# LSH attention and two feed-forwards: the feed-forwards in passes of 512 tokens instead of 768, with the gemms two steps apart

## The chip, the cores and the metric

One core of a Trainium2 chip. The metric is the device time of one execution in microseconds, the median of three runs.

## What is computed

Attention over 2 batches, 8 heads, 768 tokens and a head size of 64, in which a query sees the keys that hash to its own bucket; then two feed-forwards over all 1536 tokens, 512 to 2048 to 512 features, the first with a sigmoid-approximated gelu, the second with mish. All in fp32.

```python
mask = q_bucket[:, :, :, None] == k_bucket[:, :, None, :]
scores = np.where(mask, scale * np.matmul(q, k.transpose(0, 1, 3, 2)), -1e9)
attn = np.exp(scores - np.max(scores, axis=-1, keepdims=True))
x = np.matmul(attn / attn.sum(-1, keepdims=True), v)      # heads side by side: 1536 x 512
h = x @ w_in;  x = (h * (1 / (1 + np.exp(-1.702 * h)))) @ w_out
h = x @ w2_in; x = (h * np.tanh(log1p(exp(h)))) @ w2_out
```

## The kernel before

The order of every engine's instructions is written out by hand; no scheduler moves anything. Each value that a gemm of the feed-forward takes is split in two parts, hi (rounded to the type fp32r, in which TensorE multiplies) and lo (the rest, rounded too), and a product is three matmuls: hi by hi, hi by lo, lo by hi.

**Attention** runs in 96 steps (`NSTEP`), 16 heads of 6 blocks of 128 queries. A step does the scores of one block (`qk`, L355, PE), a clamp with its row minimum (`clamp`, L368, DVE), the exponential (`expo`, L379, ACT), and for an earlier step six transposes (`trp`, L414, PE), their hi and lo parts (L421 on ACT, L426 on DVE) and the product with v (`pv`, L438 and L439, PE). POOL prepares the operands of heads to come, and for each pair of heads sums and scales the output (`x_out`, L462 and L463) and splits it (`x_split`, x_hi and L469 for x_lo) into the x tiles of the feed-forward. `at(step, f)` hangs such extra work on a step.

**Weights** come as 64 tiles of 128 x 512, 32 for each feed-forward: for each f of 16 (blocks of 128 of the 2048 hidden features) one tile for each gemm. They are loaded as 64-bit numbers (`wload`, L101, issued by SP, three raw buffers) and made into hi and lo by `wsplit`: a scaled copy on ACT (L110), three integer instructions on DVE (L112, L114, L116), a rounding on ACT (L125) and a subtraction on DVE (L127; on POOL for tiles made under attention). `wgo(k, n)` issues the next n of these six for tile k. The first `NPRE` = 3 tiles are made under attention, one per 12 steps, the others by the steps of the feed-forward, as `conv` says: two per step in the first pass over the tokens and again in the second pass, where the tiles of the second feed-forward take the place of the first one's.

**A feed-forward** (m = 0, 1) makes two passes (b), one per batch of 768 tokens, of 16 steps (f). A step computes `gemm_in` (L159): h, 128 hidden features by 768 tokens, in two banks of 384 columns (`ps_h`, two buffers); then `act`: the activation twice on ACT (L590 rounded to gh, L591 in place) and gl on DVE (L592), which is what frees the bank; then `gemm_out` of the step before, which adds to six y banks. In the first feed-forward w is the stationary operand and the tokens move, 512 (L619) and 256 (L622) columns at a time, 24 matmuls; in the second gh and gl are stationary and w moves (L608), 18 matmuls of 512 columns. After the last f, y is copied out: into x_hi and x_lo of the next feed-forward (`x_next`), or stored (`y_store`). The two halves of h of step 0 are computed between the last steps of attention, in eight parts.

The last pair of heads of attention has its `x_out` and `x_split` in the first steps of the feed-forward; its tokens are needed in the second pass.

Of the kernel before, what the change touches and what calls it, by code (L numbers as in the profile page):

```python
# [36 lines left out]
def lsh_attention_moe_kernel(  # L37
# [18 lines left out]
    HS = S // 2  # L56
    NW0 = 1
    XO = 11
    NPRE = 3
# [20 lines left out]
    xpool = ctx.enter_context(tc.tile_pool(name="xpool", bufs=2 * B))  # L80
# [3 lines left out]
    for b in range(B):  # L84
        x_hi.append(xpool.tile([P, KD, S], F32R, tag="x", name="x_hi"))
        x_lo.append(xpool.tile([P, KD, S], F32R, tag="x", name="x_lo"))
# [17 lines left out]
    def wsplit(k, sub):  # L104
# [13 lines left out]
        pi = 0 if f < NW0 + (j == 0) else 1 if f < NW1 else 2  # L118
        nb = (NW0, NW1 - NW0, KF - NW1)[pi]
        if j == 0 and pi < 2:  # L120
            nb += 1 - 2 * pi
# [22 lines left out]
    steps = [(m, b, f) for m in range(2) for b in range(B) for f in range(KF)]  # L144
# [3 lines left out]
    def gemm_in(i, t, k0=0, k1=KD):  # L148
        m, b, f = steps[i]
        if k0 == 0:  # L150
            h_t[i, t] = mps["h"].tile([P, HS], F32, tag="h", name="h")
        h = h_t[i, t]
        wh, wl = w_t[m, f, 0]
        ct = slice(t * HS, (t + 1) * HS)
        n = 3 * k0
        for kk in range(k0, k1):
            wk = slice(kk * P, (kk + 1) * P)
            for a, x in ((wh, x_hi[b]), (wh, x_lo[b]), (wl, x_hi[b])):
                nc.tensor.matmul(  # L159
                    h, a[:, wk], x[:, kk, ct], start=(n == 0), stop=(n == 3 * KD - 1)  # L160
                )
                n += 1

    def attention():
        with ExitStack() as es:
# [359 lines left out]
            for i in range(NSTEP + PVLAG):  # L525
                if i == NSTEP:
                    es_s.close()
                    mps["h"] = ctx.enter_context(
                        tc.tile_pool(name="ps_h", bufs=2, space=PSUM, side="right")
# [32 lines left out]
                for part in range(max(0, 2 * (i - NSTEP)), min(2 * (i - NSTEP) + 2, 2 * KD)):  # L562
                    gemm_in(0, part // KD, part % KD, part % KD + 1)
# [6 lines left out]
    def moe():  # L570
        with ExitStack() as es:
            gp = es.enter_context(tc.tile_pool(name="gp", bufs=2))
            wpools[1] = es.enter_context(tc.tile_pool(name="w1", bufs=NW1 - NW0))
            ps_y = es.enter_context(tc.tile_pool(name="ps_y", bufs=1, space=PSUM))
            NH = KF * B
            N = len(steps)
            A0, A1 = 512, S - 512
# [3 lines left out]
            def act(i, t):  # L581
                if t == 0:
                    gh = gp.tile([P, S], F32R, tag="gh", name="gh")
# [76 lines left out]
            for i in range(N + 1):  # L660
                if i == NH:
                    load_table(SET_MISH)
# [93 lines left out]
```

## Time and profile before

| | us |
|---|---|
| median of 3 runs | 794.1 (793.56 to 794.52) |
| the profiled execution, its time | 795.07 |
| the profiled execution, its span | 793.3 |
| PE busy in it | 767.4 |
| DVE, ACT, POOL busy in it | 443.2, 400.3, 175.4 |

Attention takes the first 250 us, the two feed-forwards the rest. The busy time of PE contains overlap: a matmul is shown from its start to its modelled end, and the next one starts before that. What a matmul costs is read from the distance of two starts. The granted clock is the share of 2.4 GHz at which TensorE ran in a stretch; it is 1.00 nearly everywhere.

### The profile page before, as it was taken

Reading aid. Unit: us, or ns where it says so; the run is one execution under the profiler, and the core shown is the slowest. Engines: PE = TensorE matmul, PEld = TensorE weight load, DVE = VectorE, ACT = ScalarE, POOL = GpSimd, SP = SyncE. Lnnn points to the kernel's source line nnn. Section 1 sums busy time; section 2 is a strip of 40 time slices with the busy share of each in tenths; the row PEclk is TensorE's granted clock in tenths of the full one; section 3 lists DMA queues with packets and bytes.
Section 4 is the critical chain, followed back from the end, with each engine's and each line's share of the span. In section 5 each row is a group of like instructions: output and inputs, shape, how many; then the busy total and the mean of one; then the engine's idle time right before and its main releaser. Section 6 shows DMA issues by size and latency. Waiting matters only on the chain.

```text
span 793.3 us, 11713 instructions
## 1 busy us (share of the span) xinstructions
PE 767.4 (97%) x4336; PEld 705.2 (89%) x4336; DVE 443.2 (56%) x861; ACT 400.3 (50%) x864; POOL 175.4 (22%) x155
## 2 busy tenths in 40 slices
PE   5999999999997999999999999999999999999998
PEld 4999999887786999999999999999999899899996
DVE  6888888889986966765277677671111112111111
ACT  5889888887887545444344454461212213122122
POOL 7867867765821200000000000000000000000000
PEclk9999999999999899999999999999999999999999
DMA  6464464654220433333034333300000002000002
GB/s 164 133 159 109 133 153 123 160 157 128 62 67 21 159 132 114 128 133 107 1 107 133 133 119 122 131 28 1 1 0 1 1 1 80 0 1 1 1 1 79
DMA packets 23977, 65.13 MB, mean 82 GB/s; under 512 B 4048, under 2 KB 6192, under 8 KB 23920
## 3 DMA queue, kind: packets, MB, share of 16 engines
q1 hardware_dynamic: 23920, 64.39, 27.4%
q8 instruction: 34, 0.56, 0.3%
q14 instruction: 23, 0.19, 0.1%
HBM read 49.38 MB, written 3.19 MB: 66 GB/s over the span
## 4 chain that ended last, share of the span: by engine, by line
PE 85%; ACT 7%; DVE 3%; issue 2%; DMA 2%; POOL 1%; SPq 0%; DVEq 0%; ACTq 0%; POOLq 0%
PE h L159 34%; PE y L608 17%; PE y L619 11%; PE y L622 6%; PE pt L414 5%; PE s L355 5%; ACT p L379 3%; ACT pth L421 3%; PE u L438 2%; PE u L439 2%; PE prep L266 2%; DVE ptl L426 1%; POOL qx L254 1%; DVE p L368 1%; DMA kn<-in_kt_dram 1%
## 5 line engine op out<-in xcount | busy, mean ns | idle before, releaser
L592 DVE TENSOR_TENSOR gl<-h,gh 128x384 fp32r<-128x384 f32 x128 | 71.3, 557 | 290.2 <-ACT h L591 290.0
L590 ACT ACTIVATE gh<-h 128x384 fp32r<-128x384 f32 x128 | 63.0, 492 | 325.0 <-PE h L159 325.0
L159 PE MATMUL h<-x_hi,wh 128*128 128x384 f32 x512 | 172.7, 337 | 5.3 <-DVE gl L592 5.3
L159 PE MATMUL h<-x_hi,wl 128*128 128x384 f32 x512 | 172.5, 337 | 0.0
L159 PE MATMUL h<-x_lo,wh 128*128 128x384 f32 x512 | 172.4, 337 | 0.0
L426 DVE TENSOR_TENSOR ptl<-pt,pth 128x384 fp32r<-128x384 f32 x192 | 97.8, 550 | 31.5 <-ACT pth L421 31.1
L159 PEld LDWEIGHTS h<-x_hi,wh 128*128 128x128 f32 x512 | 97.0, 189 | 8.1 <-DVE gl L592 5.6
L159 PEld LDWEIGHTS h<-x_lo,wh 128*128 128x128 f32 x512 | 97.0, 190 | 1.2
L159 PEld LDWEIGHTS h<-x_hi,wl 128*128 128x128 f32 x512 | 97.0, 189 | 0.0
L379 ACT ACTIVATE p<-p,mn 128x768 f32<-128x768 f32 x96 | 90.5, 943 | 12.1 <-DVE p L368 11.9
L421 ACT CAST pth<-pt 128x384 fp32r<-128x384 f32 x192 | 82.6, 483 | 23.6 <-PE pt L414 22.8
L414 PE MATMUL pt<-ident,p 128*128 128x128 f32 x576 | 84.8, 276 | 7.7 <-DVE ptl L426 4.0
L368 DVE TENSOR_SCALAR_CACHE_REDUCE p<-s 128x768 f32<-128x768 f32 x96 | 90.1, 940 | 0.4 <-PE s L355 0.3
L414 PEld LDWEIGHTS pt<-ident,p 128*128 128x128 f32 x576 | 67.0, 140 | 20.4 <-ACT p L379 8.3
L608 PE MATMUL y<-wh,gl 128*128 128x512 f32 x192 | 75.3, 392 | 0.0
L608 PE MATMUL y<-wl,gh 128*128 128x512 f32 x192 | 75.2, 392 | 0.0
L608 PE MATMUL y<-wh,gh 128*128 128x512 f32 x192 | 74.7, 389 | 0.0
L438 PE MATMUL u<-pth,vv 128*128 128x384 f32 x192 | 65.6, 341 | 0.9 <-ACT ul L456 0.9
L439 PE MATMUL u<-ptl,vv 128*128 128x384 f32 x192 | 64.6, 337 | 0.0
L591 ACT ACTIVATE h<-h 128x384 f32<-128x384 f32 x128 | 62.4, 488 | 0.0
L355 PE MATMUL s<-kh,qx 128*128 128x384 f32 x192 | 56.0, 372 | 0.0
L355 PE MATMUL s<-kb,qb 128*128 128x384 f32 x192 | 50.2, 341 | 0.2 <-ACT kb L320 0.2
(91 smaller groups left out, 1247.7 us busy)
## 6 DMA issues: line engine op xcount, KB each, us to landing
raw<-in_wt_dram SPq DMA_DIRECT2D x64, 512.0 KB, 3.2
kn<-in_kt_dram SPq DMA_DIRECT2D x16, 384.0 KB, 6.1
qn<-in_qt_dram SPq DMA_DIRECT2D x16, 192.0 KB, 4.5
vn<-in_vt_dram SPq DMA_DIRECT2D x8, 384.0 KB, 5.2
rb<-scr SPq DMA_DIRECT2D x16, 192.0 KB, 3.4
out_dram<-ob SPq DMA_DIRECT2D x12, 256.0 KB, 2.1
qx<-qk_m SPq DMA_DIRECT2D x15, 192.0 KB, 3.3
qb<-qk_m SPq DMA_DIRECT2D x15, 192.0 KB, 2.7
```

Of the source, the lines that this page charges most:

```text
L159: nc.tensor.matmul(h, a[:, wk], x[:, kk, ct], start=(n == 0), stop=(n == 3 * KD - 1))
L355: nc.tensor.matmul(s[:, f, :HS], a[:, c], bb[:, f * HS : (f + 1) * HS], start=st, stop=not st,)
L368: nc.vector.tensor_scalar(sb, s[:, :, :HS], NEG, None, ALU.min, ALU.min, accum_out=mn)
L379: nc.scalar.activation(p, p, AF.Exp, bias=mn, scale=-1.0, accum_out=z_t[n][:, t : t + 1],)
L414: nc.tensor.transpose(ptile[:, j * P : (j + 1) * P], p_t[3 * g + j][:, t * P : (t + 1) * P], ident,)
L421: nc.scalar.copy(hi, ptile[:, :HS])
L426: nc.vector.tensor_sub(lo, ptile[:, :HS], rnd(hi))
L438: nc.tensor.matmul(ut[:, :HS], vv[:, t, :], hi, start=(t == 0), stop=False)
L439: nc.tensor.matmul(ut[:, :HS], vv[:, t, :], lo, start=False, stop=(t == NT - 1))
L592: nc.vector.tensor_sub(gl[:, ct], h, rnd(gh[:, ct]))
L608: nc.tensor.matmul(y[j], x[:, tj], w, start=(first and n == 0), stop=(last and n == 2))
L619: nc.tensor.matmul(y0, w[:, wj], x[:, :A0], start=(first and n == 0), stop=(last and n == 2))
```

## The change

The feed-forwards take the 1536 tokens in three passes of 512 (`CH`, `NCH`). A step's h is one bank of 512 columns, and there are four such banks; y is four banks of 512. Every matmul of the feed-forward has 512 columns: 12 for the first gemm and 12 for the second, in 96 steps. The second gemm runs two steps behind the first (`OLAG`), and the first gemms of steps 0 and 1 are computed between the last steps of attention. Five weight tiles are made under attention, from steps 32, 44, 56, 68 and 80 (before: three, from 56, 68 and 80). In the feed-forward the first pass makes two tiles per step in a new interleaving, the third pass three per two steps. `x_split` cuts a batch where a pass begins or ends, at 512 tokens of the first batch and 256 of the second, so that it issues four POOL instructions instead of two.

```diff
+    CH = 512
+    NCH = NTOK // CH
...
-    NPRE = 3
+    NPRE = 5
...
-        wlist += [(m, 0, 0), (m, 1, 0)]
+        wlist += [(m, 0, 0), (m, 1, 0), (m, 2, 0)]
         for f in range(KF):
-            wlist += [(m, f, 1)] + [(m, f + 2, 0)] * (f + 2 < KF)
+            wlist += [(m, f, 1)] + [(m, f + 3, 0)] * (f + 3 < KF)
...
-    steps = [(m, b, f) for m in range(2) for b in range(B) for f in range(KF)]
+    steps = [(m, c, f) for m in range(2) for c in range(NCH) for f in range(KF)]
...
-            h_t[i, t] = mps["h"].tile([P, HS], F32, tag="h", name="h")
+            h_t[i] = mps["h"].tile([P, CH], F32, tag="h", name="h")
...
-            for a, x in ((wh, x_hi[b]), (wh, x_lo[b]), (wl, x_hi[b])):
+            for a, x in ((wh, x_hi[c]), (wh, x_lo[c]), (wl, x_hi[c])):
                 nc.tensor.matmul(
-                    h, a[:, wk], x[:, kk, ct], start=(n == 0), stop=(n == 3 * KD - 1)
+                    h, a[:, wk], x[:, kk], start=(n == 0), stop=(n == 3 * KD - 1)
                 )
...
-                pcopy(x_hi[b][:, hp], ul)
-                nc.gpsimd.tensor_sub(x_lo[b][:, hp], ul, rnd(x_hi[b][:, hp]))
+                t0, t1 = b * S, (b + 1) * S
+                while t0 < t1:
+                    c, o = divmod(t0, CH)
+                    n = min(CH - o, t1 - t0)
+                    xh = x_hi[c][:, hp, o : o + n]
+                    src = ul[:, t0 - b * S : t0 - b * S + n]
+                    pcopy(xh, src)
+                    nc.gpsimd.tensor_sub(x_lo[c][:, hp, o : o + n], src, rnd(xh))
+                    t0 += n
...
-                        tc.tile_pool(name="ps_h", bufs=2, space=PSUM, side="right")
+                        tc.tile_pool(name="ps_h", bufs=4, space=PSUM, side="right")
...
-                    gemm_in(0, part // KD, part % KD, part % KD + 1)
+                    gemm_in(part // KD, part % KD, part % KD + 1)
...
-            gp = es.enter_context(tc.tile_pool(name="gp", bufs=2))
+            gp = es.enter_context(tc.tile_pool(name="gp", bufs=3))
...
+            OLAG = 2
...
+            act(0)
+            wgo(conv(2)[0], 1)
+            for i in range(2, N + OLAG):
...
+                if i < N:
+                    gemm_in(i)
+                k1, k2 = (conv(i) + [None, None])[:2]
+                if k1 is not None:
+                    wgo(k1, 2)
+                    for k in conv(i - 1)[1:]:
+                        wgo(k, 1)
+                    wgo(k1, 1)
+                    wfetch(k1 + 4)
...
+                if i - 1 < N:
+                    act(i - 1)
+                if k2 is not None:
+                    wgo(k2, 1)
+                if k1 is not None:
+                    wgo(k1, 1)
+                if k2 is not None:
+                    wgo(k2, 2)
+                if k1 is not None:
+                    wgo(k1, 1)
+                if k2 is not None:
+                    wgo(k2, 1)
+                    wfetch(k2 + 4)
+                for k in conv(i + 1)[:1]:
+                    wgo(k, 1)
+                if k2 is not None:
+                    wgo(k2, 1)
+                gemm_out(i - OLAG)
```

`gemm_out` of the change has one loop for both feed-forwards: for j of 4, three matmuls of 512 columns into y[j], w stationary in the first, gh and gl in the second; `act` works on 512 columns at once.

How the order moves is seen best behind attention. DVE before, from the last copy of attention's row sums on (raw, wb, wl: a weight tile on its way; gl: the activation's low part):

```order
L402 COPY zt<-prep 6x128
L112 TENSOR_SCALAR raw<-raw 128x512
L114 SCALAR_TENSOR_TENSOR raw<-wb,raw 128x512
L116 SCALAR_TENSOR_TENSOR wb<-wb,raw 128x512
L112 TENSOR_SCALAR raw<-raw 128x512
L114 SCALAR_TENSOR_TENSOR raw<-wb,raw 128x512
L592 TENSOR_TENSOR gl<-h,gh 128x384
L116 SCALAR_TENSOR_TENSOR wb<-wb,raw 128x512
L127 TENSOR_TENSOR wl<-wb,wh 128x512
L592 TENSOR_TENSOR gl<-h,gh 128x384
L127 TENSOR_TENSOR wl<-wb,wh 128x512
```

The same place of DVE in the change, where the five instructions have become L114, L116, L118, L128 and L596:

```order
L402 COPY zt<-prep 6x128
L596 TENSOR_TENSOR gl<-h,gh 128x512
L114 TENSOR_SCALAR raw<-raw 128x512
L116 SCALAR_TENSOR_TENSOR raw<-wb,raw 128x512
L118 SCALAR_TENSOR_TENSOR wb<-wb,raw 128x512
L596 TENSOR_TENSOR gl<-h,gh 128x512
L114 TENSOR_SCALAR raw<-raw 128x512
L116 SCALAR_TENSOR_TENSOR raw<-wb,raw 128x512
L128 TENSOR_TENSOR wl<-wb,wh 128x512
L118 SCALAR_TENSOR_TENSOR wb<-wb,raw 128x512
```

The gl of step 0 has moved ahead of all conversion work, and from the second tile on the wl of one tile stands between two instructions of the next.

POOL in the middle of attention, in the change, from a head's operands to the next v operand (before, x_hi and x_lo were one row of 768 columns each, and the first wl stood 24 steps later):

```order
L258 TENSOR_TENSOR qk_m<-kn,kh 64x768
L77 TENSOR_SCALAR x_hi<-ul 128x512
L475 TENSOR_TENSOR x_lo<-ul,x_hi 128x512
L77 TENSOR_SCALAR x_hi<-ul 128x256
L475 TENSOR_TENSOR x_lo<-ul,x_hi 128x256
L128 TENSOR_TENSOR wl<-wb,wh 128x512
L77 TENSOR_SCALAR vv<-vn 128x6x64
```

Two rows have become four, and the wl of the first weight tile stands behind them.

## Rows read from the trace of the kernel before

**Rows 1.** The page, part 1: busy us (share) xinstructions of each engine.

```profile
PE 767.4 (97%) x4336; PEld 705.2 (89%) x4336; DVE 443.2 (56%) x861; ACT 400.3 (50%) x864; POOL 175.4 (22%) x155
```

**Rows 2.** Waits of PE, whole span: us in total, times, longest us.

```profile
PE h L159 <- DVE gl L592: 5.3, 1, 5.3
```

**Rows 3.** Timeline of PE, both feed-forwards: start us, us, engine, line, operation, x.

```profile
286.57 0.34 PE L159 MATMUL h<-x_hi,wh 128*128 128x384 f32 x1
...
294.89 0.34 PE L159 MATMUL h<-x_hi,wh 128*128 128x384 f32 x1
...
706.45 0.39 PE L608 MATMUL y<-wh,gh 128*128 128x512 f32 x1
...
710.58 0.33 PE L159 MATMUL h<-x_hi,wh 128*128 128x384 f32 x1
```

**Rows 4.** Timeline of PE, between attention and feed-forward: start us, us.

```profile
253.34 0.27 PE L396 MATMUL prep<-ident,z 128*6 128x128 f32 x1
258.87 0.69 PE L159 MATMUL h<-x_hi,wh 128*128 128x384 f32 x1 [5.26 <-DVE gl L592]
...
264.48 0.39 PE L159 MATMUL h<-x_hi,wl 128*128 128x384 f32 x1
264.71 0.33 PE L159 MATMUL h<-x_hi,wh 128*128 128x384 f32 x1
```

**Rows 5.** Timelines of POOL, DVE and ACT over the same wait.

```profile
253.53 1.81 POOL L462 TENSOR_TENSOR ul<-ul,uh 128x768 f32<-128x768 f32 x1 [13.77 <-ACT ul L456]
...
253.86 1.76 DVE L112 TENSOR_SCALAR raw<-raw 128x512 uint32<-128x512 uint32 x1
...
254.60 0.47 ACT L590 ACTIVATE gh<-h 128x384 fp32r<-128x384 f32 x1
...
258.27 0.55 DVE L592 TENSOR_TENSOR gl<-h,gh 128x384 fp32r<-128x384 f32 x1
```

**Rows 6.** Timeline of DVE: the clamps of attention steps 43, 55, 67, 79, 91.

```profile
109.44 0.94 DVE L368 TENSOR_SCALAR_CACHE_REDUCE p<-s 128x768 f32<-128x768 f32 x1
...
137.76 0.95 DVE L368 TENSOR_SCALAR_CACHE_REDUCE p<-s 128x768 f32<-128x768 f32 x1
...
168.61 0.95 DVE L368 TENSOR_SCALAR_CACHE_REDUCE p<-s 128x768 f32<-128x768 f32 x1
...
201.03 0.95 DVE L368 TENSOR_SCALAR_CACHE_REDUCE p<-s 128x768 f32<-128x768 f32 x1
...
232.08 0.94 DVE L368 TENSOR_SCALAR_CACHE_REDUCE p<-s 128x768 f32<-128x768 f32 x1
```

**Rows 7.** Timelines of POOL and DVE, step 73 of attention.

```profile
187.47 1.84 POOL L469 TENSOR_TENSOR x_lo<-ul,x_hi 128x768 fp32r<-128x768 f32 x1
...
187.75 2.12 DVE L116 SCALAR_TENSOR_TENSOR wb<-wb,raw 128x512 uint32<-128x512 uint32 x1
```

**Rows 8.** Timeline of DVE, one weight tile in the first feed-forward.

```profile
309.01 0.69 DVE L127 TENSOR_TENSOR wl<-wb,wh 128x512 fp32r<-128x512 f32 x1
309.62 0.42 DVE L112 TENSOR_SCALAR raw<-raw 128x512 uint32<-128x512 uint32 x1
310.14 0.70 DVE L114 SCALAR_TENSOR_TENSOR raw<-wb,raw 128x512 uint32<-128x512 uint32 x1
310.87 0.69 DVE L116 SCALAR_TENSOR_TENSOR wb<-wb,raw 128x512 uint32<-128x512 uint32 x1
311.48 0.42 DVE L112 TENSOR_SCALAR raw<-raw 128x512 uint32<-128x512 uint32 x1
```

**Rows 9.** Waits of SP's DMA queue from 257 to 345 us: total, times, longest.

```profile
SPq L101 <- DVE wb L116: 80.6, 23, 5.0
```

**Rows 10.** The page, part 6: the weight loads, KB each, median us to landing.

```profile
raw<-in_wt_dram SPq DMA_DIRECT2D x64, 512.0 KB, 3.2
```

**Rows 11.** Stretches: us, busy us (x) of PE, PEld, DVE, ACT, POOL; PEclk, DMA share, GB/s.

```profile
257.00:260.00 3.00, 1.13 (x4) 1.13 (x4) 2.90 (x5) 1.39 (x3) 1.66 (x1) 0.63 0.51 191
440.00:460.00 20.00, 20.00 (x117) 18.69 (x116) 14.40 (x27) 10.47 (x22) 0.00 (x0) 1.00 0.38 131
```

More of the change, by code (lines that the diff above doesn't have):

```diff
@@ L78, in rnd @@
         return ap.bitcast(F32)
-    xpool = ctx.enter_context(tc.tile_pool(name="xpool", bufs=2 * B))
+    xpool = ctx.enter_context(tc.tile_pool(name="xpool", bufs=2 * NCH))
     wr = ctx.enter_context(tc.tile_pool(name="wr", bufs=3))
     x_hi, x_lo = [], []
-    for b in range(B):
-        x_hi.append(xpool.tile([P, KD, S], F32R, tag="x", name="x_hi"))
-        x_lo.append(xpool.tile([P, KD, S], F32R, tag="x", name="x_lo"))
+    for c in range(NCH):
+        x_hi.append(xpool.tile([P, KD, CH], F32R, tag="x", name="x_hi"))
+        x_lo.append(xpool.tile([P, KD, CH], F32R, tag="x", name="x_lo"))
     wpools = {0: ctx.enter_context(tc.tile_pool(name="w0", bufs=NW0))}
@@ L117, in wsplit @@
         yield
[L118 to L121, printed above, removed]
+        n0 = NW0 + 3 * (j == 0)
+        pi = 0 if f < n0 else 1 if f < NW1 else 2
+        nb = (n0, NW1 - n0, KF - NW1)[pi]
         hi = wpools[pi].tile([P, DM], F32R, tag=f"wh{j}", name="wh", bufs=nb)
@@ L599, in gemm_out @@
                 if first:
-                    y_t[m, b] = [
-                        ps_y.tile([P, 512], F32, tag=f"y{j}", name=f"y{j}") for j in range(6)
-                    ]
-                y = y_t[m, b]
-                if m == 1:
-                    for j in range(NT):
-                        tj = slice(j * P, (j + 1) * P)
-                        for n, (x, w) in enumerate(((gh, wh), (gh, wl), (gl, wh))):
-                            nc.tensor.matmul(
-                                y[j], x[:, tj], w, start=(first and n == 0), stop=(last and n == 2)
-                            )
-                        if last:
-                            y_store(b, j)
-                    return
+                    y_t[m, c] = [
+                        ps_y.tile([P, CH], F32, tag=f"y{j}", name=f"y{j}") for j in range(KD)
+                    ]
@@ L614, in gemm_out @@
+                y = y_t[m, c]
                 for j in range(KD):
[L615 to L618 removed]
+                    js = slice(j * P, (j + 1) * P)
+                    for n, (x, w) in enumerate(((gh, wh), (gh, wl), (gl, wh))):
                         nc.tensor.matmul(
[L620 to L628 removed]
@@ L629, in gemm_out @@
-                    if last:
-                        x_next(b, j, slice(0, A0), y0)
-                        if j % 2:
-                            for jj in (j - 1, j):
-                                o = (jj % 2) * A1
-                                x_next(b, jj, slice(A0, S), y[KD + j // 2][:, o : o + A1])
-            def x_next(b, j, c, y):
-                nc.scalar.copy(x_hi[b][:, j, c], y)
-                nc.vector.tensor_sub(x_lo[b][:, j, c], y, rnd(x_hi[b][:, j, c]))
+                            y[j],
@@ new lines, in gemm_out @@
+                            w[:, js] if m == 0 else x[:, js],
+                            x if m == 0 else w,
+                            start=(first and n == 0),
+                            stop=(last and n == 2),
+                        )
+                    if last and m == 0:
+                        nc.scalar.copy(x_hi[c][:, j], y[j])
+                        nc.vector.tensor_sub(x_lo[c][:, j], y[j], rnd(x_hi[c][:, j]))
+                    elif last:
+                        y_store(c, j)
```

108 lines of the change are left out of this document (34 added, 74 removed).

## The prediction

> **What bounds the kernel now.** I read the page's busy times first, then PE's waits, then timelines where a wait ends or a step repeats. PE is busy 97% of the span [rows 1], so a change gains only by giving PE less work, by closing a wait of PE's, or it loses by making PE wait. Behind attention PE has one wait of size: 5.3 us, ended by DVE's gl of line 592 [rows 2]. From there to the end it runs without a gap, so the feed-forward costs what its matmuls cost. In attention PE isn't alone: a step is as long as the loop PE, ACT, DVE and back, and DVE's clamp of line 368, one per step, is the clock of that loop [rows 6].
>
> **Fewer, wider matmuls.** In the first feed-forward one step lasts from 286.57 to 294.89, 8.32 us [rows 3]: 24 matmuls of 384 columns, 12 of 512 and 12 of 256, together 18,432 columns. At 2.4 GHz these stream for 7.68 us, so 0.64 us over 48 matmuls is left, 13.3 ns each. In the second feed-forward 18 matmuls of 512 columns take from 706.45 to 710.58, 4.13 us against 3.84 of streaming: 16 ns each. The columns stay what they are. The matmuls go from 32 x 48 + 32 x 42 = 2880 to 96 x 24 = 2304. 576 fewer at 13.3 ns is **-7.7 us**, all of it on PE's path, and I take the 13.3 since most of the removed ones are of 384 and 256 columns.
>
> The Trainium skill (TensorE: Matmul & The Clock Gate, section "Wait — 56ns, not 53.3ns?") gives a warm back-to-back matmul a fixed cost of only 2.5 ns beside its columns. By that the term would be 576 x 2.5 ns = 1.4 us; the rows here show five times as much, in two kinds of step, and they decide.
>
> **The wait behind attention.** PE ends its last attention work, the small transpose of 253.34, and next starts at 258.87, after 5.26 us of idling [rows 4]. It wants an h bank; there are two, and the first is held until gl of step 0 has read it. That gl starts at 258.27, since DVE has five conversion instructions ahead of it, the first stretched to 1.76 us by a POOL instruction that began at 253.53 [rows 5] (0.42 where nothing is in the way [rows 8]). After the idling the clock is at the lower level: the 18 matmuls that start from 258.87 to 264.48 stand 5.61 us apart in all, where 17 intervals of a 384-column matmul (160 ns of streaming and 13.3) are 2.95. So the wait costs 5.26 + 2.66 = 7.9 us.
>
> After the change PE has work there: steps 0 and 1 are computed inside attention's last steps, there are four h banks, and gemm_in of step 2 (12 x 0.227 = 2.72 us) needs only a third bank and a weight tile made under attention. PE's tail of attention has 24 matmuls of 512 instead of 384 columns, 1.3 us more, so that it ends at about 254.6 on the old time scale, and gemm_in of step 2 ends at 257.3. ACT's gelu of step 0 stands directly behind the last u copies, without the two REBIAS instructions of before; they took it to 254.60 [rows 5], so even 1 us later it ends by 256, and gl(0), first in DVE's queue now, by 256.3. That is 1 us ahead of gemm_out(0). The next weight needed, second-gemm tile of step 1, is the first tile that the feed-forward makes itself; PE wants it at 262.7, two PE blocks later, and the seven DVE instructions up to its wl take 4.3 us by rows 8, out of 6. The wait goes: **-7.9 us**.
>
> **Two more weight tiles under attention.** The clamps of steps 43, 55, 67, 79 and 91 give four stretches of 12 steps [rows 6]: 28.32 us without a conversion, then 30.85, 32.42 and 31.05 with one each. So the first costs 2.53 us, the second 4.10, the third 2.73. The new ones begin 24 and 12 steps earlier, at the same place in the pattern of 12 steps (32 and 44 instead of 56). With five in a row I take the old first price for the first, the old last for the last, and the middle one three times: 2.53 + 3 x 4.10 + 2.73 = 17.56 against 9.36, +8.2 us.
>
> From this a part goes back. In step 73 L116 takes 2.12 us instead of 0.69 [rows 7, 8]: it starts 0.28 behind POOL's x_lo of line 469 and ends 0.56 behind that one's end, as if it had begun only then. The change cuts x_hi and x_lo into pieces of 512 and 256 columns. The first x_lo piece is two thirds of 1.84 us and starts some 0.25 earlier, because x_hi's piece before it is shorter: it ends about 0.8 us earlier, and L116 could run between the two pieces. I give 0.75 for each of the four conversions that meet an x_split (in the last of the old ones there was no such meeting): -3.0. Together **+5.2 us**. Ends: +8.2 if the cut helps nothing; +2.1 if the two new tiles cost the lowest seen price less the help (2 x 1.8) and the old ones get theirs (2 x 0.75).
>
> **The first pass of the feed-forward.** A step of PE shrinks from 8.32 us to 24 x 0.227 = 5.44, while two tiles per step still have to be made in it. By the starts in rows 8, DVE's instructions follow each other in 0.61 (wl), 0.52 (L112), 0.73 (L114, whose consumer is next) and 0.61 (L116). In the new order a wl stands between L114 and L116, so that I count 0.61 there: 2.35 per tile, and with 0.61 for a gl of 512 columns 5.31 us per step. DVE is then 98% full but not the bound, and the five tiles made beforehand and the two steps between the gemms absorb a late instruction. POOL's last x_out and x_split fall into the first steps and can hold DVE up. For this and for the four y banks that the next pass takes over at once from copies (a gemm_in of 2.72 us lies between) I allow **+1.5 us**. In the last pass of the first feed-forward three tiles are made per two steps, 3.5 us of DVE per 5.44; the second feed-forward makes none. The end (last copy and store) is unchanged.
>
> **Sum.** -7.7 - 7.9 + 5.2 + 1.5 = -8.9 us. The profiled execution (795.07 us, 1.8 of it outside its span of 793.3) would become 786.2. It lies 1.0 above the median of the runs, 794.1, on which the forecast is made: **785.2 us**. What a measurement can tell from no change is about 0.2%, 1.6 us.
>
> **Rivals.**
>
> *DVE becomes the bound of the first pass.* At whole durations instead of start distances a tile is 0.42 + 0.70 + 0.69 + 0.69 = 2.50 us [rows 8], a step 2 x 2.50 + 0.69 = 5.69: 0.25 over PE's 5.44, 3.3 us in 13 steps. If three of POOL's last instructions also stretch one of DVE's as in rows 5 (1.76 instead of 0.42), that is 4.0 more. Less the 1.5 allowed: 785.2 + 5.8 = 791.0. For it: DVE has only 2% left. Against: rows 8 show the overlap of neighbours. Chance 0.16.
>
> *The change doesn't close the wait.* PE stops at gemm_out(0) or (1) instead, for gl(0) or the first weight tile made late, long enough for the clock to fall as in rows 4: +7.9, 793.1 us. Against: gl(0) stands first now. Chance 0.07.
>
> *A matmul's fixed cost is no cost of the matmul.* If the 13.3 ns belonged to the columns (a weight load or an operand read that goes on beside them and grows with them), wider matmuls would keep all of it: +7.7, 792.9 us. Rows 3 speak against it, three widths with about the same rest per matmul. Chance 0.03. (The 2.5 ns of the Trainium skill, same page and section, would end near it, at 791.5 us.)
>
> *Slower: the weight loads.* The first pass needs 24 more loads of 512 KB in some 13 x 5.44 = 71 us, 177 GB/s; in steady state they ran at 131 [rows 11]. At that rate they take 24 x 0.524 MB / 131 = 96 us, PE waits 25 us in pieces, 810 us. It turns the sign where less than about 155 GB/s comes. Against: SP's loads waited 80.6 us in 23 waits for DVE to free a buffer [rows 9], so 131 is what was asked, one lands in 3.2 us [rows 10] with three buffers to turn in 8.2 us, and 191 GB/s stands in one stretch [rows 11]. Chance 0.06.
>
> **How the numbers follow.** The forecast has 0.68; its own range, from the attention ends (-3.1, +3.0) and from no stall at all (-1.5), is 781 to 788.5. With the DVE case, 0.16, it holds 0.84: 781 to 791. Faster by over 0.2% (below 792.5) are the forecast and the DVE case: 0.84. Within 0.2% are the wait that stays and the fixed-cost case: 0.10. Slower is the load case: 0.06.
>
> **What would show it.** Right, step by step: 2304 feed-forward matmuls with starts 227 ns apart and steps of 5.44 us; no PE wait over 1 us between attention and feed-forward and a granted clock of 1.00 there; stretches of 12 attention steps of 30 to 32 us from step 31 on, and a last clamp about 5 us later; L116's counterpart at 1.3 to 1.5 us instead of 2.1. Wrong: PE waits for wl or gl that repeat every step of the first pass, raw loads landing in 5 us or more, or an attention that ends over 8 us later.

## The result, and the profile after

| | before | after |
|---|---|---|
| median of 4 runs | 794.25 us (793.56 to 794.52) | 784.40 us (782.43 to 787.02) |
| ratio, 95% interval | | 0.9879 [0.9858, 0.9901] |
| the profiled execution: time, span | 795.07, 793.3 | 783.52, 781.5 |

The changed kernel is 1.2% faster, 9.9 us by the medians; 785.2 was forecast. A second set of four runs of the same kernel gave 784.04. In the profiled executions it is 11.5 us (795.07 to 783.52), since the one of the kernel before lies above its four runs and that of the changed kernel below its median. In the changed kernel the load of a raw tile stands in line 103, the three integer instructions in L114, L116 and L118, the rounding in L126, wl in L128, x_lo in L475, gl in L596, and the second gemm in L612.

The page after, part 1, against [rows 1]:

```profile
PE 758.0 (97%) x3760; PEld 642.4 (82%) x3760; DVE 434.6 (56%) x823; ACT 397.6 (51%) x796; POOL 184.4 (24%) x173
```

The 576 matmuls are gone (4336 to 3760). PE is as full as before, so the span followed PE's work and PE's waits. The waits of PE after, whole span, against [rows 2] (us in total, times, longest):

```profile
PE s L355 <- DMA kb<-mk: 1.3, 2, 1.1
PE h L159 <- DVE wl L128: 0.9, 1, 0.9
```

The wait of 5.3 us for gl has gone, and in the feed-forward one of 0.9 us for a wl has come. New, too, are the 1.3 us in attention for small transfers (kb <- mk, a mask). The clamps of steps 31, 43, 55, 67, 79, 91 and 95 (the last) in DVE's timeline after, against [rows 6]:

```profile
81.17 0.95 DVE L368 TENSOR_SCALAR_CACHE_REDUCE p<-s 128x768 f32<-128x768 f32 x1
...
111.26 0.95 DVE L368 TENSOR_SCALAR_CACHE_REDUCE p<-s 128x768 f32<-128x768 f32 x1
...
142.92 0.95 DVE L368 TENSOR_SCALAR_CACHE_REDUCE p<-s 128x768 f32<-128x768 f32 x1
...
174.56 0.94 DVE L368 TENSOR_SCALAR_CACHE_REDUCE p<-s 128x768 f32<-128x768 f32 x1
...
206.38 0.94 DVE L368 TENSOR_SCALAR_CACHE_REDUCE p<-s 128x768 f32<-128x768 f32 x1
...
236.55 0.95 DVE L368 TENSOR_SCALAR_CACHE_REDUCE p<-s 128x768 f32<-128x768 f32 x1
...
246.42 0.95 DVE L368 TENSOR_SCALAR_CACHE_REDUCE p<-s 128x768 f32<-128x768 f32 x1
```

The last clamp of before stood at 241.71. So attention ends **4.7 us later**, and what follows it takes 781.5 - 246.42 = 535.1 us instead of 793.3 - 241.71 = 551.6: **16.5 us less**. Together -11.8, the difference of the two spans.

A step of PE in each feed-forward, from one step's first matmul of the second gemm to the next one's (timeline of PE after):

```profile
301.63 0.39 PE L612 MATMUL y<-gh,wh 128*128 128x512 f32 x1
...
307.07 0.39 PE L612 MATMUL y<-gh,wh 128*128 128x512 f32 x1
...
704.19 0.39 PE L612 MATMUL y<-wh,gh 128*128 128x512 f32 x1
...
709.63 0.39 PE L612 MATMUL y<-wh,gh 128*128 128x512 f32 x1
```

Both are 5.44 us for 512 tokens, 8.16 for 768. In the first feed-forward a step of 768 tokens took 8.32 [rows 3]. In the second it took 8.31, from this row of the kernel before to the 710.58 of [rows 3]:

```profile
702.27 0.33 PE L159 MATMUL h<-x_hi,wh 128*128 128x384 f32 x1
```

Over 32 steps each that is 5.1 + 4.8 = 9.9 us of the 16.5. The other 6.6 us lie between attention and the feed-forward, where PE's timeline after answers to [rows 4]:

```profile
258.84 0.40 PE L159 MATMUL h<-x_hi,wl 128*128 128x512 f32 x1
259.07 0.27 PE L396 MATMUL prep<-ident,z 128*6 128x128 f32 x1
259.10 0.48 PE L159 MATMUL h<-x_hi,wh 128*128 128x512 f32 x1
...
261.94 0.39 PE L612 MATMUL y<-gh,wh 128*128 128x512 f32 x1
...
270.10 0.39 PE L159 MATMUL h<-x_hi,wh 128*128 128x512 f32 x1
...
271.57 0.50 PE L159 MATMUL h<-x_hi,wl 128*128 128x512 f32 x1 [0.86 <-DVE wl L128]
...
277.15 0.39 PE L159 MATMUL h<-x_hi,wh 128*128 128x512 f32 x1
```

Behind the small transpose the first gemm of step 2 goes on at once, and at 261.94 the second gemm of step 0 follows. The next rows are those of DVE and POOL over the stretch, against [rows 5]:

```profile
260.50 0.69 DVE L596 TENSOR_TENSOR gl<-h,gh 128x512 fp32r<-128x512 f32 x1 [0.84 <-ACT h L595]
...
264.77 2.33 DVE L128 TENSOR_TENSOR wl<-wb,wh 128x512 fp32r<-128x512 f32 x1
...
269.74 1.78 DVE L128 TENSOR_TENSOR wl<-wb,wh 128x512 fp32r<-128x512 f32 x1
```

```profile
264.43 2.13 POOL L463 TENSOR_TENSOR ul<-ul,rb 128x768 f32<-128x768 f32 x1 [3.67 <-DMA rb<-scr]
...
269.36 1.61 POOL L475 TENSOR_TENSOR x_lo<-ul,x_hi 128x512 fp32r<-128x512 f32 x1
```

gl of step 0 ends 0.75 us before PE wants it. Then two of DVE's wl meet POOL's instructions and last 2.33 and 1.78 us instead of 0.69: the second one is the wait of 0.86. That step takes 7.05 us (270.10 to 277.15) instead of 5.44, and the two ahead of it 0.1 us too much: the first pass loses 1.7 us, and every later step takes 5.44. In the kernel before, the wait took 5.3 us and the step behind it 11.06 (258.87 to 269.93) instead of 8.32, 8.0 us lost in all, so 6.3 of the 6.6 us are accounted for. The stretches of the first pass (as in [rows 11]) show how full DVE is:

```profile
260.00:280.00 20.00, 19.04 (x83) 15.06 (x82) 18.77 (x27) 10.70 (x19) 7.04 (x6) 1.00 0.40 140
280.00:300.00 20.00, 20.00 (x90) 16.57 (x89) 19.17 (x35) 13.71 (x24) 0.00 (x0) 1.00 0.60 189
300.00:320.00 20.00, 20.00 (x90) 16.54 (x90) 19.27 (x35) 13.30 (x24) 0.00 (x0) 1.00 0.60 207
```

DVE is busy 96% and PE 100%, and the loads run at up to 207 GB/s: neither the DVE rival nor the load rival came about.

### The profile page after: what moved, and what is told of

Read it like the earlier page. It is cut to its first block, busy times and chain, and to the rows that moved or that the text cites. A ratio compares the mean times of both kernels' runs of the same rounds, so it can differ in the third digit from the quotient of the medians.

```text
span 781.5 us, 10532 instructions
## 1 busy us (share of the span) xinstructions
PE 758.0 (97%) x3760; PEld 642.4 (82%) x3760; DVE 434.6 (56%) x823; ACT 397.6 (51%) x796; POOL 184.4 (24%) x173
## 4 chain that ended last, share of the span: by engine, by line
PE 79%; DVE 6%; ACT 5%; DMA 3%; POOL 3%; issue 3%; SPq 1%; DVEq 0%; POOLq 0%; ACTq 0%
PE y L612 33%; PE h L159 32%; PE s L355 4%; PE pt L414 4%; ACT p L379 2%; PE u L438 2%; PE u L439 2%; ACT pth L421 2%; PE prep L266 2%; POOL qx L254 1%; DMA vn<-in_vt_dram 1%; DMA kb<-mk 1%; DVE ptl L426 1%; DVE p L368 1%; DVE z L391 1%
## 5 line engine op out<-in xcount | busy, mean ns | idle before, releaser
L596 DVE TENSOR_TENSOR gl<-h,gh 128x512 fp32r<-128x512 f32 x96 | 66.2, 690 | 267.2 <-ACT h L595 266.8
L594 ACT ACTIVATE gh<-h 128x512 fp32r<-128x512 f32 x96 | 57.3, 597 | 256.1 <-PE h L159 255.5
L159 PE MATMUL h<-x_hi,wl 128*128 128x512 f32 x384 | 149.6, 389 | 0.9 <-DVE wl L128 0.9
L159 PE MATMUL h<-x_hi,wh 128*128 128x512 f32 x384 | 149.5, 389 | 0.0
L159 PE MATMUL h<-x_lo,wh 128*128 128x512 f32 x384 | 149.4, 389 | 0.0
L426 DVE TENSOR_TENSOR ptl<-pt,pth 128x384 fp32r<-128x384 f32 x192 | 97.8, 550 | 30.7 <-ACT pth L421 30.2
L159 PEld LDWEIGHTS h<-x_hi,wl 128*128 128x128 f32 x384 | 72.1, 188 | 16.3 <-DVE wl L128 1.3
L159 PEld LDWEIGHTS h<-x_lo,wh 128*128 128x128 f32 x384 | 72.0, 188 | 14.7
L612 PE MATMUL y<-gh,wl 128*128 128x512 f32 x192 | 74.8, 390 | 0.1
L612 PE MATMUL y<-gh,wh 128*128 128x512 f32 x192 | 74.7, 389 | 0.0
L612 PE MATMUL y<-wh,gh 128*128 128x512 f32 x192 | 74.7, 389 | 0.0
L612 PE MATMUL y<-wl,gh 128*128 128x512 f32 x192 | 74.7, 389 | 0.0
L612 PE MATMUL y<-gl,wh 128*128 128x512 f32 x192 | 74.7, 389 | 0.0
L612 PE MATMUL y<-wh,gl 128*128 128x512 f32 x192 | 74.7, 389 | 0.0
## 6 DMA issues: line engine op xcount, KB each, us to landing
out_dram<-ob SPq DMA_DIRECT2D x12, 256.0 KB, 2.0
```

What stands on the lines that cost most here:

```text
L159: nc.tensor.matmul(h, a[:, wk], x[:, kk], start=(n == 0), stop=(n == 3 * KD - 1))
L426: nc.vector.tensor_sub(lo, ptile[:, :HS], rnd(hi))
L594: nc.scalar.activation(gh, h, fn)
L596: nc.vector.tensor_sub(gl, h, rnd(gh))
L612: nc.tensor.matmul(y[j], w[:, js] if m == 0 else x[:, js], x if m == 0 else w, start=(first and n == 0), stop=(last and n == 2),)
```

## The experiments

Eleven further kernels were run, and the changed kernel once more. Each ratio is against the kernel before, run beside it. The ranges behind the medians are the lowest and highest run.

### Does the cost belong to the matmul or to its columns?

`e2_halves_second_ff`: the changed kernel, with the first gemm of the second feed-forward in halves, the same columns in 576 more matmuls.

```diff
-                nc.tensor.matmul(h, a[:, wk], x[:, kk], start=..., stop=...)
+                for o in (0, 256) if m else ():
+                    nc.tensor.matmul(h[:, o : o + 256], a[:, wk], x[:, kk, o : o + 256], start=..., stop=...)
+                if m == 0:
+                    nc.tensor.matmul(h, a[:, wk], x[:, kk], start=..., stop=...)
```

> The changed kernel, with each matmul of the first gemm of the second feed-forward (576 of 512 columns, a part in which no weight tile is made) cut into two of 256: 576 matmuls more, the same columns. Theory (13.3 ns for each matmul whatever its width): a step of the second feed-forward goes from 5.44 to 5.60 us, the run is 7.7 us longer than the changed kernel, about 792. Rival (2.5 ns for each matmul, the rest belongs to the columns): 1.4 us longer. Second rival (at 256 columns the load of the stationary operand, 188 ns long, no longer hides beside the stream): more than 15 us longer.

Measured: 791.64 us, median of ten (six from 791.27 to 791.75, four from 794.44 to 796.21), ratio 0.9984 [0.9967, 1.0000]. Against the changed kernel's two medians, 784.40 and 784.04, that is 7.2 to 7.6 us, 12.6 to 13.2 ns for each matmul more. In the profiled execution the part behind the last clamp is 8.6 us longer, 14.9 ns each. All of it is near the 13.3 ns of the sum. PE's timeline splits a step of the second feed-forward (L160 is the first gemm here, L621 the second):

```profile
707.40 0.40 PE L160 MATMUL h<-x_hi,wh 128*128 128x256 f32 x2
...
710.27 0.40 PE L621 MATMUL y<-wh,gh 128*128 128x512 f32 x1
...
713.02 0.40 PE L160 MATMUL h<-x_hi,wh 128*128 128x256 f32 x2
```

The 24 matmuls of 256 columns take 2.87 us, 0.15 more than the 12 wide ones (12 x 0.227 = 2.72). The 12 of the second gemm, which nobody touched, take 2.75, 229 ns each instead of 227, as beside the gemm of 384 columns in the kernel before (229 [rows 3]). So a second gemm is slower beside a narrower first one. A cost of columns would have given nothing here, and it is ruled out. The Trainium skill (TensorE: Matmul & The Clock Gate, section "Wait — 56ns, not 53.3ns?") states 2.5 ns for each matmul, an estimate of 1.4 us for this edit; the trace does not agree, 7.2 to 8.6 us. In this kernel every matmul has a weight load of its own (3760 of each in the page after); no run here has matmuls without one. Why four runs lie 3 us higher stays open.

### What does the cut of x_split give?

`e5_cut_x_split`: the kernel before, with `x_split` cut as in the change.

```diff
-                pcopy(x_hi[b][:, hp], ul)
-                nc.gpsimd.tensor_sub(x_lo[b][:, hp], ul, rnd(x_hi[b][:, hp]))
+                cut = 512 if b == 0 else 256
+                for o in (slice(0, cut), slice(cut, S)):
+                    xh = x_hi[b][:, hp, o]
+                    pcopy(xh, ul[:, o])
+                    nc.gpsimd.tensor_sub(x_lo[b][:, hp, o], ul[:, o], rnd(xh))
```

> The kernel before, with only x_split cut as in the change: per pair of heads four POOL instructions of 512 and 256 columns instead of two of 768. Theory (a DVE instruction with two SBUF inputs that meets a POOL instruction runs when that one ends, and it gets in between two POOL instructions): L116 of the first two tiles made under attention takes 1.3 to 1.5 us instead of 2.13 and 2.12; the stretches of 12 steps from clamp 55 and 67 are 0.7 us shorter each, the third the same; the run 1.5 us shorter. Rival (DVE waits for POOL's whole piece of work, or POOL's two more instructions push the next operands back): the stretches are the same or longer, 0 to +1 us.

Measured: 792.37 us (nine runs), ratio 0.9977 [0.9966, 0.9989], 1.8 us faster. The stretches from step 55 to 67 and from 67 to 79 shrink by 0.74 and 1.37 us. The timelines of POOL and of DVE, steps 61 and 73, against [rows 7]:

```profile
155.42 1.29 POOL L472 TENSOR_TENSOR x_lo<-ul,x_hi 128x512 fp32r<-128x512 f32 x1
...
186.89 0.74 POOL L472 TENSOR_TENSOR x_lo<-ul,x_hi 128x256 fp32r<-128x256 f32 x1
```

```profile
155.90 1.36 DVE L116 SCALAR_TENSOR_TENSOR wb<-wb,raw 128x512 uint32<-128x512 uint32 x1
...
187.58 0.68 DVE L116 SCALAR_TENSOR_TENSOR wb<-wb,raw 128x512 uint32<-128x512 uint32 x1
```

At step 61 L116 starts inside the x_lo piece and ends 0.55 us behind it, so it has only a piece to wait for and not the whole (1.36 us where it took 2.13 before); at step 73 the shorter piece comes first, L116 starts 0.05 us before that ends, and takes 0.68. The Trainium skill (SBUF — State Buffer, section "SBUF: two separate sides") says that a DVE instruction with both inputs in SBUF and a GpSimd instruction that reads SBUF exclude each other for a whole instruction; the rows agree, 2.12 us against 0.68. The mechanism of the forecast stands: the cut helps by the length of what L116 has to wait for.

`e6_third_stage_later`: the changed kernel with L118 one step later, behind the x_split.

```diff
-                for off in (-1, 0, 2, 5, 8, 9):
+                for off in (-1, 0, 2, 6, 8, 9):
```

> The changed kernel, with the last integer instruction (DVE L118) of the five weight tiles made under attention one step later, offset 6 instead of 5, where POOL has ended its x_split and sits idle for 8 us. Theory (0.65 us of each tile's price is L118 meeting x_split): L118 takes 0.69 us in all five tiles, each of the four stretches that hold a meeting now gets 0.65 us shorter, attention ends 2.6 us earlier, about 782 us. Rival (the price is DVE's and ACT's own work, the meeting only falls into a step that has slack elsewhere): within 0.5 us of the changed kernel.

Measured: 784.94 us (783.57 to 785.61), ratio 0.9876 [0.9862, 0.9891]: no gain. L118 took 0.75 us as forecast, and the first three stretches became shorter, by 0.4, 0.8 and 0.55 us. The last two became longer, by 0.5 and 1.9: PE waited 1.5 us there for a small transfer (s from kb <- mk), and a DVE instruction met one of POOL, of which more below. The 782 of the forecast was missed.

### What closes the wait behind attention?

`e1_gelu_first`: the kernel before, with both activations of step 0 ahead of the loop, and so ahead of the conversions on ACT and DVE.

```diff
+            act(0, 0)
+            act(0, 1)
             wgo(conv(0)[0], 1)
...
-                    act(i, 0)
+                    if i:
+                        act(i, 0)
...
-                    act(i, 1)
+                    if i:
+                        act(i, 1)
```

> The kernel before, with only the order behind attention changed: both activations of step 0 (ACT) and both gl (DVE) are issued ahead of the first two weight tiles; two h banks, the gemms one step apart and passes of 768 tokens stay. Theory (the wait has two causes: gl stands behind conversion work, and DVE has about 8 us of work before the second step's banks come free, part of it held up by POOL): the 5.3 us wait shrinks to 1 to 2 us, but a new wait of 1.5 to 4 us appears within the next 12 us, for gl of step 1 or a weight tile; gain 2.5 to 6 us, 788 to 792 us. Rival (the order alone was the cause): no second wait, gain 6 to 8 us, 786 to 788 us, which would leave nothing of that term to the four banks and the two-step lag.

Measured: 793.44 us (ten runs), ratio 0.9989 [0.9980, 0.9998]. PE's idling shrank to 1.6 + 0.3 us and the clock stayed at 1.00, yet hardly anything was gained. The edit had a side effect: since `act` had taken step 0's h away, the loop computed step 0's first gemm a second time, 24 matmuls of 384 columns, 4.2 us of PE. Two rows of its PE, the start of step 2's first gemm and of what follows it, are needed below:

```profile
268.96 0.45 PE L159 MATMUL h<-x_hi,wh 128*128 128x384 f32 x1 [0.32 <-DVE gl L592]
...
273.24 0.39 PE L619 MATMUL y<-gh,wh 128*128 128x512 f32 x1
```

This run didn't decide, and the edit was made again without the second computation.

`e1b_gelu_first_once`: the same, with step 0's first gemm computed once.

```diff
-                        if (i, t) not in h_t:
+                        if i and (i, t) not in h_t:
```

> The kernel before, with both activations of step 0 issued ahead of the loop and with step 0's first gemm computed once (the earlier run of this edit computed it twice). Theory (the wait behind attention is 5.3 us of idle time plus 2.7 us at the lower clock, and its cause is that the activations stand behind the conversions): the waits h <- gl around 254 to 262 us shrink to under 2 us, the granted clock stays at 1.00, and the time falls by 2.5 to 6 us against before, to 788 to 791.5; what is missing to 7.9 us shows as new waits of PE on weight conversions within the next 10 us. Rival (the wait is only moved, since DVE has the same work to do before the second step can go on): under 1 us gained, 793.5 to 794.3, with as much PE idle between 254 and 275 us as before.

Measured: 795.39 us (ten runs), ratio 1.0011 [1.0001, 1.0020]. My theory fell and its rival held: nothing is gained. The timeline of PE in this run:

```profile
255.30 0.45 PE L159 MATMUL h<-x_hi,wh 128*128 128x384 f32 x1 [1.61 <-DVE gl L592]
...
268.37 0.57 PE L159 MATMUL h<-x_hi,wh 128*128 128x384 f32 x1 [4.47 <-DVE gl L592]
...
274.24 0.39 PE L619 MATMUL y<-gh,wh 128*128 128x512 f32 x1
```

The wait is 1.61 us at the old place and 4.47 us one step later, 6.1 in all, and again the clock is low behind it: the granted clock from 268 to 272 is 0.57, most of that stretch at the lower level (1.2 GHz), and the 24 matmuls from 268.37 on take 5.87 us. From the last clamp (241.78) to the end it is 793.4 - 241.78 = 551.6 us, as before. DVE shows why; its timeline in between:

```profile
259.15 2.15 DVE L116 SCALAR_TENSOR_TENSOR wb<-wb,raw 128x512 uint32<-128x512 uint32 x1
261.22 3.56 DVE L127 TENSOR_TENSOR wl<-wb,wh 128x512 fp32r<-128x512 f32 x2
264.70 0.42 DVE L112 TENSOR_SCALAR raw<-raw 128x512 uint32<-128x512 uint32 x1
...
267.76 0.55 DVE L592 TENSOR_TENSOR gl<-h,gh 128x384 fp32r<-128x384 f32 x1
```

DVE has the two gl done by 256.0 and then works nearly without a gap on the conversions that they overtook. gl of step 1 comes at 267.76. The wait isn't made by the place of gl in the queue: it is conversion work that DVE owes, and it is paid at one place or at the next. A large part of the debt falls together with POOL's work: L116 and the two L127 take 5.7 us instead of three times 0.69, 3.6 us more, while POOL does the last x_out and x_split from 258.42 to 264.22. No run moves that work of POOL out of the kernel before, so how much of the wait would go with it is open.

The first run fits in: its 4.2 us of needless matmuls and 1.9 us of idling are the same 6.1 us. Counted from the last clamp (242.36 there), PE begins step 2's first gemm at the same point, 26.6 us, in both. But there the granted clock is 1.00, and the 24 matmuls from 268.96 on take 4.28 us instead of 5.87. These 1.6 us are the whole difference behind the last clamp (550.0 against 551.6). Against the kernel before beside it, that run is 1.0 us faster and this one 0.8 slower, with 24 matmuls fewer.

Does the change then close the wait by its order, or by the two tiles it makes beforehand? `e3_three_tiles` and `e4_four_tiles` are the changed kernel with three and four tiles under attention, and the rest at the head of the feed-forward, behind the activation of step 0.

```diff
-    NPRE = 5
+    NPRE = 3
...
             act(0)
+            for k in range(NPRE, 5):
+                wgo(k, 6)
+                wfetch(k + 4)
```

> The changed kernel with three weight tiles made under attention, as before, instead of five; the other two are made by DVE and ACT at the head of the feed-forward, behind the activation of step 0. Theory (two tiles cost attention 5 to 6 us and spare the first pass, in which DVE is 98% full, 4.7 us of DVE work that it can't make up): the last clamp comes 5 to 6 us earlier, PE waits 4 to 6 us in the first steps of the feed-forward and its clock falls there for some us (2 to 3 us more); in all 0 to +3 us against the changed kernel. Rival (the first pass has room for two tiles): no new wait over 2 us, 3 to 5 us faster than the changed kernel.

> The changed kernel with four weight tiles made under attention; the fifth is made at the head of the feed-forward. Theory: the last clamp comes 2.5 to 3.4 us earlier, PE waits 2 to 3 us more in the first steps, with or without a fall of the clock: -1 to +2 us against the changed kernel. Rival (room in the first pass): 2 to 3 us faster.

Measured: three tiles 782.04 us (781.93 to 784.27), ratio 0.9852 [0.9837, 0.9867]; four tiles 787.22 us (783.79 to 788.41), ratio 0.9904 [0.9879, 0.9928]. Run beside the changed kernel (784.04), three tiles are 2.0 us faster where 0 to 3 slower was expected, and four are 3.2 us slower where at most 2 was: both times missed. The profiled execution of three tiles shows the mechanism that was expected; it is the slowest of its four, 784.27. The last clamp comes 5.1 us earlier than with five, at 241.33, and what follows it is 6.1 us longer. PE's waits in that stretch, from 245 to 300 us:

```profile
PE y L612 <- ACT wh L126: 1.8, 1, 1.8
PE y L612 <- DVE wl L128: 1.4, 2, 1.2
PE h L159 <- DVE wl L128: 1.0, 1, 1.0
```

With one more of 0.2 they are 4.4 us, and the granted clock from 260 to 265 is 0.66. With four tiles the profiled execution (787.78) waits 3.6 us there, at a clock of 0.50 from 270 to 275, while its last clamp comes only 1.0 us earlier than with five: one stretch of attention took 34.13 us, with an L114 of 1.92 and an L116 of 2.23 in it.

`e9_three_tiles_combined` has three tiles and the two edits of the next part, and makes the other two ahead of the activation of step 0.

> The changed kernel with three weight tiles under attention and two at the head of the feed-forward, the last piece of the last x_split on ScalarE and VectorE, and the raw loads two steps later. Theory by the single runs (three tiles: 2 us by medians; the late piece: 0.7; the late transfers: up to 3 in some runs): 779 to 782. Rival (the first pass has no slack left for the two tiles, and the pieces collide): 782 to 785, as with each edit alone.

Measured: 784.29 us (782.84 to 785.47), ratio 0.9869 [0.9854, 0.9884]. Its last clamp and PE's wait, in the timelines of DVE and of PE (L618 is the second gemm here, L600 the activation that makes gh):

```profile
239.01 0.95 DVE L368 TENSOR_SCALAR_CACHE_REDUCE p<-s 128x768 f32<-128x768 f32 x1
```

```profile
261.15 0.79 PE L618 MATMUL y<-gh,wh 128*128 128x512 f32 x1 [6.47 <-ACT gh L600]
```

Against `e8_load_behind_masks` below, with five tiles, the last clamp comes 7.1 us earlier (246.08 to 239.01), and the part behind it is 7.0 us longer (535.0 to 542.0), in a wait of 6.5 us with the clock low behind it (0.56 from 260 to 265). Here the order has a part in the wait: ACT's gh stands behind the roundings of the two tiles, which wait for DVE. So the four banks and the two steps between the gemms alone do not close the wait: without the two tiles it is back at 4.4 to 6.5 us. Whether they are needed with five tiles was not tested. The rows after only give an estimate: gl ends at 261.19, and without the first gemm of step 2 ahead of it PE would want it at about 259.1, 2 us earlier. The two tiles cost about the same in either place: by the runs three tiles are 2.0 us faster in one pair (`e3_three_tiles`, `after_again`) and 1.5 us slower in the other (`e9_three_tiles_combined`, `e10_five_tiles_combined`).

### What spreads the runs of the changed kernel?

`after_again`: the changed kernel once more, with a profile.

> The changed kernel once more, as the yardstick on the same chip: 782 to 787 us; its runs lie further apart than those of the kernel before. Theory: the wait at step 4 of the first pass is just long enough that the clock falls in some executions and not in others.

Measured: 784.04 us (782.69 to 785.15), ratio 0.9866 [0.9848, 0.9883]. Its last clamp came 1.8 us later than in the first profile, and what follows it took 535.0 us as there (535.1), so this spread lies in attention and not where I had expected it. PE's timeline in this run:

```profile
202.81 0.84 PE L355 MATMUL s<-kb,qb 128*128 128x384 f32 x2 [1.16 <-DMA kb<-mk]
```

The first profile has the same wait, 1.09 us. Behind it the steps fall out of their pattern: step 80 took 3.15 us there and 4.77 here. DVE and POOL show the difference, first in the first profile, then in this one:

```profile
211.39 0.42 DVE L114 TENSOR_SCALAR raw<-raw 128x512 uint32<-128x512 uint32 x1
211.40 2.11 POOL L462 TENSOR_TENSOR ul<-ul,uh 128x768 f32<-128x768 f32 x1
```

```profile
211.19 2.03 DVE L114 TENSOR_SCALAR raw<-raw 128x512 uint32<-128x512 uint32 x1
211.09 1.83 POOL L462 TENSOR_TENSOR ul<-ul,uh 128x768 f32<-128x768 f32 x1
```

L114 started 0.01 us ahead of POOL's instruction there. Here it started 0.10 behind it and ended 0.3 behind its end. Six other profiles agree. In `e3_three_tiles` and `e6_third_stage_later`, with waits of 1.5 us, L114 also started behind (0.3 and 0.5 us) and took 1.8 and 1.65; the stretch from step 79 to 91 took 32.1 to 32.5 us in these three. In `e4_four_tiles`, `e7_late_piece_off_pool`, `e8_load_behind_masks` and `e10_five_tiles_combined`, with waits of 0.5 us or less at this place, L114 started 0.8 us ahead and took about 1.0; that stretch took 30.7 to 30.8. In the first profile it took 30.2, with the wait of 1.09. So the wait alone did not lengthen the stretch; where L114 had fallen behind POOL's instruction it was 1.3 to 2.3 us longer. That the late transfer is what makes L114 fall behind fits these eight profiles, but no run changes the place of L114 alone. On SP's queue the small mk transfers (48 KB each, issued from 196.48 on) stand right behind a raw weight load of 512 KB (194.94).

`e7_late_piece_off_pool` takes the last POOL piece of the first pass (the 512 columns that hold up a wl at 269.74) to ACT and DVE, four steps later.

```diff
+                    if only == "end" and c == NCH - 1:
+                        nc.scalar.copy(xh, src)
+                        nc.vector.tensor_sub(xl, src, rnd(xh))
...
-            late.append(lambda: x_split(NHD // 2 - 1))
+            late.append(lambda: x_split(NHD // 2 - 1, "head"))
+            late.append(lambda: x_split(NHD // 2 - 1, "end"))
...
-                if i < KF and i in (4, 6):
+                if i < KF and i in (4, 6, 8):
```

> The changed kernel, with the 512-column piece of the last pair's x_split taken from POOL and done by ACT and DVE at step 8 (it is read in the third pass only). Theory (PE's one wait in the first pass, 0.9 us for wl at step 4, comes from DVE's instructions that meet POOL's last x_out and x_split, among them a wl of 1.78 us that meets this piece): the meeting of 1.78 us goes, the wait shrinks to under 0.3 us, no later wait takes its place; 0.5 to 1.3 us faster than the changed kernel, and TensorE's clock stays at 1.00. Rival (DVE is full, so work put on it at step 8 comes out as a wait there): the same total.

Measured: 783.32 us (782.66 to 785.60), ratio 0.9867 [0.9849, 0.9884]. The wait for wl shrank from 0.9 to 0.3 us; the time can't be told from that of the changed kernel, 784.04 beside it.

`e8_load_behind_masks` issues the raw load two steps later, behind the mk transfers; `e10_five_tiles_combined` is that and the edit of `e7_late_piece_off_pool`.

```diff
-                at(st + 6, wfetch, k + 4)
+                at(st + 8, wfetch, k + 4)
```

> The changed kernel with the raw weight loads under attention issued two steps later (8 steps behind a tile's start instead of 6), so that on SP's queue they stand behind the four small transfers qb/kb <- mk and not ahead of them. Theory (the runs of the changed kernel spread from 782.4 to 787.0 because the small transfers land late behind the 512 KB load in some executions, some 3 us each time): no wait s <- kb of PE over 1 us, step 80 at 3.8 us instead of 4.4 to 4.8 in the profiled run, and runs that cluster within 1.5 us at 781.5 to 783.5. Rival (the late landing comes from the vn, qn and kn transfers, 960 KB, which stay where they are): the same spread, 782.4 to 787.

> The changed kernel with five weight tiles under attention as it has them, the last piece of the last x_split on ScalarE and VectorE, and the raw loads two steps later. Theory: 780.5 to 782.5 with a spread under 1.5 us. Rival (the loads are not what spreads the runs): 782 to 786.

Measured: 782.93 us (782.69 to 783.74), ratio 0.9855 [0.9840, 0.9869], and 782.82 us (782.81 to 783.41), ratio 0.9853 [0.9839, 0.9868]. In the first of the two the wait of PE is this row of its timeline:

```profile
202.27 0.76 PE L355 MATMUL s<-kb,qb 128*128 128x384 f32 x2 [0.17 <-DMA kb<-mk]
```

The first kept its forecast; the second came out 0.3 us above its own (780.5 to 782.5), and nothing was added by the two edits together. The runs cluster as the theory said: eight runs with the load behind lie from 782.7 to 783.7, the eight of the changed kernel from 782.4 to 787.0, four of them above 785. The kn, vn and qn transfers stayed where they were, which speaks against the rival. Two things stay open. The changed kernel was not run beside these two, and `e9_three_tiles_combined`, which has the load behind as well, spreads from 782.84 to 785.47, at mean clocks of 0.993 to 0.996, so its long wait may be what spreads it. With four runs each the gain in the median, some 1.3 us, is within the intervals. No version of the eleven is beyond doubt faster than the changed kernel; `e3_three_tiles`, `e8_load_behind_masks` and `e10_five_tiles_combined` have the best ratios, 0.985, and can't be told apart.

## Why the prediction came out right

- **Fewer matmuls, -7.7 forecast, -9.9 measured.** The price of 13.3 ns held: 5.1 us in the first feed-forward as the sum had it. In the second I counted the removed matmuls at 13.3 ns as well, but the step there fell from 8.31 to 8.16 us, 4.8 us in all where 192 matmuls at 13.3 ns are 2.6. The 16 ns of the second gemm [rows 3] went to 13.3 once the first gemm beside it had 512 columns too, and I had left them as they were. `e2_halves_second_ff` goes the way back: with halves beside it the second gemm is at 16 ns again, which makes 14.9 ns per matmul added.
- **The wait and the stalls, -7.9 + 1.5 = -6.4 forecast, -6.6 measured.** The sizes held: 8.0 us lost before, 1.7 after. The cause that I gave was wrong: "it stands behind five conversion instructions" is where the wait showed. `e1b_gelu_first_once` put gl first and the same time came back one step later, 13 us on.
- **Two more tiles, +5.2 forecast, +4.7 measured at the last clamp.** By stretches of 12 steps: 30.09, 31.66, 31.64, 31.82 and 30.17 us, which is 13.8 over five times 28.32, where I had 17.56 - 3.0 = 14.6. L118 takes 1.33 to 1.35 us where it meets an x_split in the first three, as forecast, and 0.68 in the last two.
- **The two terms are one.** The sum counted the wait and the tiles as independent, a gain and a cost. The runs with three tiles show that closing the wait is what the two tiles buy: -6.6 + 4.7 is a net of 1.9 us. Of the 11.8 us between the two profiles, 9.9 is the matmuls. The cut of x_split alone gave the kernel before 1.8 us (`e5_cut_x_split`, with a last clamp 1.6 us earlier), so by these numbers next to nothing is left for the tiles, the banks and the lag together; no run takes them apart. The sum came out because the change has both edits. For three tiles the same working would drop the +8.2 and keep the help of the cut for two tiles (-1.5), 778.5 us; 782.0 and 784.3 were measured.
- **What was luck.** The forecast was worked out on the profiled execution, 786.2, and that came out at 783.5, 2.7 us off, of which 2.2 is the matmul term. On the medians it is only 0.8 us off, since the profiled execution lay 1.0 above the median before and 0.9 below it after, in runs that spread by 4.6 us. (The upper end of the range, 788.5, is 788.2 by its own terms.)
- **The rivals.** DVE as the bound: 96% full in the first pass, and PE waits for it only in the first 15 us of the feed-forward. The wait that stays came about only where the two tiles were taken away. The cost that is none of the matmul was ruled out by `e2_halves_second_ff`. The loads: 207 GB/s were given, and the median landing went from 3.2 [rows 10] to 3.3 us.

## What to carry to other kernels

A wait for an engine that has been busy for some time before it can be a debt of work, which shows at one place or at the next: count what that engine has to do until the consumer's next needs, not what stands directly ahead. Moving the consumer's instruction forward moved the wait here; making some of the work earlier paid for it elsewhere, and both prices have to be read before one calls it a gain. What lasted was less work for the engine that is 97% full.

## What the runs showed of the hardware

- A matmul with a weight load of its own cost 13 to 14 ns beside its columns at 256, 384 and 512 columns. At 512 columns it was 16 ns beside a gemm of 384 or 256, in code that was the same: a removed narrow matmul can be worth more than its own cost (4.8 us for 192 in the second feed-forward).
- 24 needless matmuls, 4.2 us, that kept PE from idling made the part behind attention 1.6 us shorter than idling in their place, because the granted clock stayed at 1.00 instead of falling to 0.57 in the stretch behind the wait: the next 24 matmuls took 4.28 instead of 5.87 us.
- Four transfers of 48 KB behind a load of 512 KB on the same queue landed in 4.7 to 5.7 us, and PE waited 1.1 to 1.2 us for them; with the load issued behind them they landed in 4.2 us in one run and 2.6 in the other, and PE waited 0.17 us and not at all.
- An integer instruction of DVE with one input (L114) took 0.42 us when it started 0.01 us ahead of a POOL instruction, and 2.03 when it started 0.10 us behind it.
